# Two token blocks taken through half the hidden features each in turn, with the first layer's weights converted in pairs

## The chip, the cores and the metric

The kernel runs on one core of a Trainium2 chip. The metric is device time in microseconds (us), the median of repeated runs; smaller is better. Engines are called as in the profile: PE (matrix products) with PEld (its weight loads), DVE (vector), ACT (scalar, activations), POOL (GpSimd) and SP (here only a queue that starts DMA transfers). PSUM holds the results of PE, SBUF everything else.

## The reference, cut to what matters

```python
# q, k, v: (8, 8, 576, 64) float32; weights arrive as 64-bit floats
scores = q_c @ k_c.T / 8           # in chunks of 64 tokens
attn = softmax(scores)
x = (attn @ v_c)                   # -> (4608, 512)
h = x @ w_in                       # (512, 2048)
g = maximum(h, 0) + alpha * minimum(h, 0)
x = g @ w_out                      # (2048, 512)
h = x @ w_in2
g = h - tanh(h)
out = g @ w_out2                   # (4608, 512) float32
```

## The kernel before, in words

4608 tokens are cut into 9 blocks of 512 (`NB`), the 2048 hidden features into 16 groups of 128 (`KF`), f = 0 to 15. A **step** is one f of one block. The program runs the 9 blocks through layer 1, then the 9 blocks through layer 2: 288 steps.

Each step has two halves on PE, 12 matmuls of 128x512 each. `up` (L417) multiplies the block's input by the group's slice of w_in into one PSUM bank (`hps`). `down` (L476) multiplies the activated group by its slice of w_out and adds into four PSUM banks (`y`), which collect all 16 groups. `down` of f stands two steps after `up` of f (`LAG = 2`, a queue). For accuracy every factor is kept as a high and a low part, and a half is three products: high times high, low times high, high times low.

Between the halves stand, in layer 1: two ACT operations (`neg`, L432, and `g`, L433), a DVE operation that joins them (L434), then the split of g: the high part on ACT (`ghi`, L446), the low part on POOL or DVE (`glo`, L449).

The weights arrive as 64-bit floats, which no engine here computes with. A slice is called a piece, (f, 0) for w_in and (f, 1) for w_out, 128x512 numbers; layer 1 has 32. A piece is loaded by SP and turned into float32 by two ACT operations (`wm`, `scrh` or `scrl` at L106, `wr` at L107) and four DVE operations (L117, L121, L123, L127; together the conversion). Then it is split: high part on ACT (L152), low part on POOL (L153). All of layer 1's pieces are converted while block 0 runs, two pieces a step. Layer 2's pieces are converted during the later blocks of layer 1, written to device memory ("parked") and fetched before layer 2.

Attention works on tiles of 128 tokens, four to a block. Tiles 0 to 3 are done ahead of step 0, later tiles beside the steps: score matmuls (L284), maximum and subtraction on DVE (L313, L316), exponential on ACT (L319), sum and reciprocal on DVE (L325 to L328), the multiplication on POOL (L329), transposition and copies (L334, L343 on DVE, L344 on ACT), the product with v (L355), and the split of the result into the block's input (`xh` L397 on ACT, `xl` L401 on DVE).

The order: most of the program is written in the order in which each engine is to run it (`manual_schedule`); a table (`at`, `fire`) hangs attention, loads and conversions on step numbers. Only the steps of block 0 (`step_first`) are ordered by the framework's scheduler; `step_one` serves the other blocks of layer 1, `step_two` layer 2. An engine takes its instructions strictly in its order and waits where one isn't ready.

At a block's end `finish` copies the four banks by ACT into tiles `yst` of the pool `stage` (7 buffers of 128x512, shared with many other tiles) and SP writes them to device memory; layer 2 reads them back as `yraw`.

Of the kernel before, what the change touches and what calls it, by code (L numbers as in the profile page):

```python
# [11 lines left out]
I32 = mybir.dt.int32  # L12
# [15 lines left out]
def kernel(  # L28
# [32 lines left out]
    stage = ctx.enter_context(tc.tile_pool(name="stage", bufs=7))  # L61
# [18 lines left out]

    wsplit = {}

    def slot(f, which, shape, dtype):
        return wpool.tile(shape, dtype, tag=f"w{which}_{f}", name=f"w{which}_{f}")

    def load_raw(raw, layer, f, which, h=0):
        src = ((w_in1, w_out1), (w_in2, w_out2))[layer][which]
        n = raw.shape[1]
        if which == 0:
            nc.sync.dma_start(  # L90
                out=raw.rearrange("p (kk m) -> p kk m", m=P),
                in_=src[h * n:(h + 1) * n, f * P:(f + 1) * P].rearrange(
                    "(kk p) m -> p kk m", p=P),
            )
        else:
            nc.sync.dma_start(out=raw, in_=src[f * P:(f + 1) * P, h * n:(h + 1) * n])

    def to_f32_a(raw, m):
# [6 lines left out]
        r = stage.tile([P, 512], I32, tag="st", name="wr")[:, :raw.shape[1]]  # L105
# [23 lines left out]
    def new_w():  # L129
        return stage.tile([P, 512], F32, tag="st", name="wm")  # L130

    raw_w, w32 = {}, {}

    def load_w(f, which):
        raw_w[f, which] = slot(f, which, [P, 512], I64)
        load_raw(raw_w[f, which], 0, f, which)

    scratch, w_parts = [], {}

    def convert_a(*pieces):  # L140
# [6 lines left out]
    def convert_b(*pieces, ops=(0, 1, 2, 3)):
        to_f32_b([w_parts[piece] for piece in pieces], ops)

    def split_w(f, which, lo_engine):  # L150
        w, w_ = w32.pop((f, which)), slot(f, which, [P, 2, 512], F32R)
        nc.scalar.activation(out=w_[:, 0], in_=w, func=AF.Copy)  # L152
        lo_engine.tensor_tensor(out=w_[:, 1], in0=w, in1=w_[:, 0].bitcast(F32), op=ALU.subtract)  # L153
        wsplit[f, which] = w_

    parked, park_raw, park_t = {}, {}, {}

    def park_load(f, which, h):
        park_raw[f, which, h] = stage.tile([P, 256], I64, tag="st", name="rw")
        load_raw(park_raw[f, which, h], 1, f, which, h)  # L160

    def park_convert(f, which, h):
        if h == 0:
            park_t[f, which] = new_w()
        to_f32_b([to_f32_a(park_raw.pop((f, which, h)), park_t[f, which][:, h * 256:(h + 1) * 256])])

    def park_store(f, which):
        parked[f, which] = dram.tile([P, 512], F32, name=f"w2_{which}_{f}")
        nc.sync.dma_start(out=parked[f, which], in_=park_t.pop((f, which)))

    def fetch_w(f, which):
        w32[f, which] = new_w()
        nc.sync.dma_start(out=w32[f, which], in_=parked[f, which])
# [12 lines left out]
    def load_v(t, f=None):  # L186
        vt = slot(f[0], f[1], [P, H, D], F32) if f else vpool.tile([P, H, D], F32, tag="v", name="v")
# [66 lines left out]
    def att_a_early(t, i):  # L254
        tr = ps_y.tile([P, HP, P], F32, tag=f"y{i}", name="tr")
# [53 lines left out]
    def att_e(t, early=False):  # L309
# [4 lines left out]
        pool, tag = (stage, "st") if early else (att, "p")  # L314
        p = pool.tile([P, H, D], F32, tag=tag, name="p")
# [48 lines left out]
    def att_t_early(t):  # L364
# [5 lines left out]
        pts[t] = stage.tile([P, HP, P], F32, tag="st", name="pte")  # L370
        return nc.scalar.activation(out=pts[t], in_=tr, func=AF.Copy)
# [97 lines left out]
    def down(layer, f, g, acc, cuts=((0, 4),)):  # L469
        w = wsplit[f, 1]  # L470
        for c0, c1 in cuts:
            for i, (u, x) in enumerate(((0, 0), (1, 0), (0, 1))):
                for t in range(c0, c1):
# [3 lines left out]
                        out=acc[t], lhsT=lhsT, rhs=rhs, start=(f == 0 and i == 0), stop=(f == KF - 1 and i == 2)  # L477
# [7 lines left out]
    ysc = {}  # L485

    def finish(layer, j, t0, acc, ends=False):
        if layer == 0:
            ysc[j] = dram.tile([KD, P, NB], F32, name=f"ysc{j}")
        for i, a in enumerate(acc):  # L490
            st = stage.tile([P, 512], F32, tag="st", name="yst")
            if i % 2 == 0 or not ends:
# [324 lines left out]
```

## Time and profile before

| | us |
|---|---|
| median of 3 runs (lowest to highest) | 1712.93 (1711.82 to 1713.32) |
| the profiled execution's own time | 1713.04 |
| its span, first to last instruction | 1711.3 |
| PE busy | 1660.6 (97%) |
| DVE busy | 1300.3 (76%) |
| ACT busy | 837.4 (49%) |
| POOL busy | 354.2 (21%) |

The busy share is a mean over stages. The span in 40 slices of 43 us shows PE at nine tenths or more nearly everywhere but in the first four slices, where DVE is at nine tenths and the granted TensorE clock dips. So the views by stretch, by wait and in order of time are read for the first 185 us apart from the rest.

### The profile page before, as it was taken

The numbers are of one execution on the slowest core, as the hardware profiler recorded it, in microseconds if no ns is written. First come the engines' busy times: TensorE is split into PE (matmuls) and PEld (weight loads), VectorE is DVE, ScalarE is ACT, GpSimd is POOL, SyncE is SP. The second block draws the span as 40 slices with busy tenths as digits, with TensorE's granted clock in tenths as the row PEclk, the third lists the DMA queues.
The fourth block names the chain that finished last, engine by engine and source line by source line (L and its number), as shares of the span: only waits on it lengthen the run. The fifth ranks groups of instructions, "written<-read, shape, count | busy, mean of one in ns | idle before, by whom it ended". The sixth has DMA issues, their size and how long they took to land.

```text
span 1711.3 us, 25017 instructions
## 1 busy us (share of the span) xinstructions
PE 1660.6 (97%) x9389; PEld 1365.2 (80%) x9389; DVE 1300.3 (76%) x2000; ACT 837.4 (49%) x1593; POOL 354.2 (21%) x265
## 2 busy tenths in 40 slices
PE   7876899999999999999999999999999999999998
PEld 6664787888888888888888888888888888888887
DVE  7998465766576765664245999999999999999987
ACT  6575444555555545454355444444444444444443
POOL 2654100000000000000054322222222222222221
PEclk9897899999999999999999999999999999999999
DMA  9821323343253333430233010101010100000000
GB/s 247 255 59 28 72 69 87 93 106 87 58 121 75 102 85 93 99 88 18 94 89 108 1 50 1 50 1 50 1 50 1 41 10 27 23 19 32 6 20 25
DMA packets 215593, 108.60 MB, mean 63 GB/s; under 512 B 170912, under 2 KB 187312, under 8 KB 215472
## 3 DMA queue, kind: packets, MB, share of 16 engines
q1 hardware_dynamic: 215472, 107.01, 23.4%
q8 instruction: 73, 1.20, 0.3%
q14 instruction: 48, 0.39, 0.1%
HBM read 79.70 MB, written 27.26 MB: 63 GB/s over the span
## 4 chain that ended last, share of the span: by engine, by line
PE 83%; DVE 7%; issue 5%; POOL 2%; ACT 1%; SPq 1%; DMA 1%; POOLq 0%; DVEq 0%; ACTq 0%
PE y L476 40%; PE hps L417 40%; POOL w L153 2%; PE sc L284 1%; SPq L231 1%; PE sc L355 1%; DVE g L434 1%; DVE wm L123 1%; DVE wm L117 1%; DVE scrh L117 1%; DVE wm L127 0%; DVE scrh L123 0%; DMA wm<-w 0%; DVE wm L121 0%; DVE scrl L123 0%
## 5 line engine op out<-in xcount | busy, mean ns | idle before, releaser
L417 PE MATMUL hps<-xh,w 128*128 128x512 f32 (+1 forms) x2312 | 578.6, 392 | 11.5 <-ACT xh L397 9.2
L417 PEld LDWEIGHTS hps<-xh,w 128*128 128x128 f32 x2312 | 436.1, 189 | 103.6 <-ACT xh L397 9.5
L449 POOL TENSOR_TENSOR glo<-g,ghi 128x512 fp32r<-128x512 f32 x160 | 214.1, 1338 | 604.1 <-ACT ghi L446 560.5
L476 PE MATMUL y<-ghi,w 128*128 128x512 f32 x1152 | 304.8, 400 | 8.7 <-ACT ghi L446 5.1
L417 PE MATMUL hps<-xl,w 128*128 128x512 f32 (+1 forms) x1156 | 309.0, 389 | 0.0
L476 PE MATMUL y<-w,ghi 128*128 128x512 f32 x1152 | 293.7, 389 | 1.4 <-ACT ghi L446 1.3
L458 ACT ACTIVATE sq<-hps 128x512 f32<-128x512 f32 x144 | 86.2, 598 | 417.0 <-PE hps L417 416.1
L434 DVE SCALAR_TENSOR_TENSOR g<-neg,nalpha_sb,g 128x512 f32<-128x512 f32 x144 | 115.5, 802 | 206.9 <-ACT g L433 206.9
L476 PEld LDWEIGHTS y<-ghi,w 128*128 128x128 f32 x1152 | 216.7, 191 | 57.4 <-ACT ghi L446 6.1
L476 PEld LDWEIGHTS y<-w,ghi 128*128 128x128 f32 x1152 | 216.0, 188 | 47.4 <-ACT ghi L446 2.7
L417 PEld LDWEIGHTS hps<-xl,w 128*128 128x128 f32 x1156 | 217.3, 188 | 45.2
L465 DVE SCALAR_TENSOR_TENSOR g<-w,g 128x512 f32<-128x512 f32 x144 | 242.3, 1682 | 0.0
L446 ACT ACTIVATE ghi<-g 128x512 fp32r<-128x512 f32 x288 | 181.8, 631 | 85.1 <-DVE g L434 72.6
L432 ACT ACTIVATE neg<-hps 128x512 f32<-128x512 f32 x144 | 85.9, 597 | 213.3 <-PE hps L417 203.5
L329 POOL TENSOR_TENSOR p<-p,rd 128x512 f32<-128x512 f32 x35 | 44.6, 1274 | 604.8 <-DVE rd L328 602.4
L476 PE MATMUL y<-glo,w 128*128 128x512 f32 x576 | 163.9, 392 | 0.0
L476 PE MATMUL y<-w,glo 128*128 128x512 f32 x576 | 162.8, 389 | 0.0
L476 PEld LDWEIGHTS y<-glo,w 128*128 128x128 f32 x576 | 109.4, 190 | 23.2
L476 PEld LDWEIGHTS y<-w,glo 128*128 128x128 f32 x576 | 108.1, 188 | 22.8 <-DVE glo L449 0.4
L466 DVE SCALAR_TENSOR_TENSOR g<-sq,g 128x512 f32<-128x512 f32 x144 | 111.3, 773 | 5.0
L467 DVE COPY_PREDICATED g<-ktc,th 128x512 f32<-128x512 uint32 x144 | 109.7, 762 | 4.9
L449 DVE TENSOR_TENSOR glo<-g,ghi 128x512 fp32r<-128x512 f32 x128 | 91.9, 718 | 23.5 <-ACT ghi L446 22.6
(98 smaller groups left out, 1517.8 us busy)
## 6 DMA issues: line engine op xcount, KB each, us to landing
ysc<-yst SPq DMA_DIRECT2D x36, 256.0 KB, 2.3
yraw<-ysc SPq DMA_DIRECT2D x9, 1024.0 KB, 5.9
out_dram<-yst SPq DMA_DIRECT2D x36, 256.0 KB, 2.2
w<-in_moe_w_in_dram SPq DMA_DIRECT2D x16, 512.0 KB, 6.2
w<-in_moe_w_out_dram SPq DMA_DIRECT2D x16, 512.0 KB, 6.2
rw<-in_moe_w_in_dram SPq DMA_DIRECT2D x32, 256.0 KB, 3.0
rw<-in_moe_w_out_dram SPq DMA_DIRECT2D x32, 256.0 KB, 3.1
w<-wm SPq DMA_DIRECT2D x32, 256.0 KB, 2.1
```

Of the source, the lines that this page charges most:

```text
L117: nc.vector.tensor_scalar(out=m, in0=m, scalar1=as_float(0x4FEFFFFF), scalar2=as_float(0x40000000), op0=ALU.min, op1=ALU.max)
L329: engine.tensor_tensor(out=p, in0=p, in1=rd.to_broadcast([P, H, D]), op=ALU.mult)
L417: nc.tensor.matmul(out=hp[:, cols], lhsT=w[:, a, m], rhs=x[b][:, kk, cols], start=(kk == 0 and i == 0), stop=(kk == KD - 1 and i == 2),)
L432: nc.scalar.activation(out=neg, in_=hp, func=AF.Relu, scale=-1.0)
L434: nc.vector.scalar_tensor_tensor(out=g, in0=neg, scalar=nalpha_sb[:, f:f + 1], in1=g, op0=ALU.mult, op1=ALU.add)
L446: nc.scalar.activation(out=hi, in_=g, func=AF.Copy)
L449: lo_engine.tensor_tensor(out=lo, in0=g, in1=hi.bitcast(F32), op=ALU.subtract)
L458: nc.scalar.activation(out=sq, in_=hp, func=AF.Square)
L465: nc.vector.scalar_tensor_tensor(out=g, in0=w, scalar=ce, in1=g, op0=ALU.add, op1=ALU.mult)
L466: nc.vector.scalar_tensor_tensor(out=g, in0=sq, scalar=ca, in1=g, op0=ALU.add, op1=ALU.mult)
L467: nc.vector.copy_predicated(g, mask, th)
L476: nc.tensor.matmul(out=acc[t], lhsT=lhsT, rhs=rhs, start=(f == 0 and i == 0), stop=(f == KF - 1 and i == 2))
```

## The change

The first two blocks are taken in four parts: block 0 with f 0 to 7, block 1 with f 0 to 7, block 0 with f 8 to 15, block 1 with f 8 to 15. Between its parts a block's four `y` banks are written to device memory (`finish_half`), read back (`load_half`) and added by DVE to the sums of the second part (`finish_sum`). The parts are numbered as steps 0 to 31; the steps from 32 on are as before.

The layer-1 pieces form 15 pairs (two, (0,0) and (1,0), stay single): pair d holds (d, 1) and (d+2, 0), and each operation of its conversion and split takes 1024 columns. Pair d is converted in step d for d = 0 to 7 (`step_first`, now for 8 steps), pairs 8 to 14 in steps 9, 11, ... 21 and split one step later. A pair has one place in SBUF (`home`), which in the beginning also holds data of attention. Tiles 4 to 7 are now loaded and transposed early like tiles 0 to 3 (`att_a_second`); their attention runs in steps 1 to 7. The whole program is in written order. `stage` has 3 buffers instead of 7, a pool `wide` takes tiles of 1024, `g` has two buffers of its own. Layer 2's pieces are converted whole instead of in halves, and fetched in pairs.

```diff
-    stage = ctx.enter_context(tc.tile_pool(name="stage", bufs=7))
+    stage = ctx.enter_context(tc.tile_pool(name="stage", bufs=3))
+    wide = ctx.enter_context(tc.tile_pool(name="wide", bufs=2))
...
+    PAIRS = {"s0": [(0, 0)], "s1": [(1, 0)]}
+    PAIRS.update({d: [(d, 1), (d + 2, 0)] for d in range(KF - 2)})
+    PAIRS[KF - 2] = [(KF - 2, 1), (KF - 1, 1)]
...
+    def convert_a(d):
+        raw, m = raw_w.pop(d), new_w(d).rearrange("p a n -> p (a n)")
+        r = wide.tile([P, 1024], I32, tag="r", name="wr", bufs=1)[:, :m.shape[1]]
+        w_parts[d] = to_f32_a(raw.rearrange("p a n -> p (a n)"), m, r)
...
+    def split_w(d, lo_engine):
+        w = w32.pop(d)
+        w_ = home(d, [P, len(PAIRS[d]), 2, 512], F32R, "w")
+        nc.scalar.activation(out=w_[:, :, 0], in_=w, func=AF.Copy)
+        lo_engine.tensor_tensor(out=w_[:, :, 1], in0=w, in1=w_[:, :, 0].bitcast(F32), op=ALU.subtract)
...
-                        out=acc[t], lhsT=lhsT, rhs=rhs, start=(f == 0 and i == 0), stop=(f == KF - 1 and i == 2)
+                        out=acc[t], lhsT=lhsT, rhs=rhs, start=(f == ends[0] and i == 0), stop=(f == ends[1] and i == 2)
...
+    def finish_half(j, acc):
+        spill[j] = dram.tile([KD, P, NB], F32, name=f"half{j}")
+        put_away(acc, spill[j])
...
+    def finish_sum(j, acc):
+        ysc[j] = dram.tile([KD, P, NB], F32, name=f"ysc{j}")
+        for i, (a, y) in enumerate(zip(acc, half.pop(j))):
+            nc.vector.tensor_tensor(out=y, in0=a, in1=y, op=ALU.add)
+            nc.sync.dma_start(out=ysc[j][i], in_=y)
...
-        base[t] = (3, 5, 7, 9)[t - NPT] if t < 2 * NPT else KF * (t // NPT - 1) - 4 + 4 * (t % NPT)
+        base[t] = t - 3 if t < 2 * NPT else 2 * t + 3 if t < 3 * NPT else KF * (t // NPT - 1) - 4 + 4 * (t % NPT)
...
+    for d in range(HF, KF - 1):
+        at(2 * d - 7, convert, d)
+        at(2 * d - 6, split_w, d, nc.gpsimd)
...
+    def step_first(step, j, t0, f, ends, x, acc):
+        d, t = step, chain.get(step)
+        if late:
+            split_hi(*late[0])
+        fire(step, (1,))
+        convert_a(d)
+        if t is not None:
+            att_e(t)
+        hp = up(f, x, NB, slice(2 * P, NB), hp0) if step == 0 else up(f, x, NB)
+        fire(step, (0,))
+        if len(queue) == LAG:
+            next_down()
+        if step == 0:
+            att_a_second(5)
+        if step == 1:
+            att_a_second(6)
+            att_a_second(7)
+        convert_b(d, (0,))
+        if t is not None:
+            att_n(t)
+        if late:
+            split_lo(*late.pop(), nc.gpsimd)
+        convert_b(d, (1, 2))
+        if t is not None:
+            att_t(t)
+            att_d(t)
+        convert_b(d, (3,))
+        g = act_g(0, f, hp, NB)
+        queue.append((0, f, g, acc, j, t0, ends))
+        late.append(g)
+        split_w(d, nc.gpsimd)
+        fire(step, (2, 3, 4))
...
+    parts = [(j, a, a + HF) for a in (0, HF) for j in range(2)] + [(j, 0, KF) for j in range(2, len(plan))]
+    step = 0
+    with tc.manual_schedule():
+        for j, a, b in parts:
```

**DVE, before: around the fourth step of block 0.** `scrh`, `scrl` and `wm` are pieces in conversion, `g` the activation that PE waits for.

```order
L117 TENSOR_SCALAR scrh<-scrh 128x512
L121 TENSOR_SCALAR scrh<-scrh 128x512
L123 SCALAR_TENSOR_TENSOR scrh<-w_5_156,scrh 128x512
L127 ISA scrh<-scrh,wr 128x1024
L434 SCALAR_TENSOR_TENSOR g<-neg,nalpha_sb,g 128x512
L117 TENSOR_SCALAR scrl<-scrl 128x512
L121 TENSOR_SCALAR scrl<-scrl 128x512
L123 SCALAR_TENSOR_TENSOR scrl<-w_3_161,scrl 128x512
```

**DVE, in the change: step 2, the first with a tile's attention (tile 4), between the `g` of steps 1 and 2.**

```order
L320 TENSOR_REDUCE mx<-sc 128x8
L322 TENSOR_TENSOR p<-sc,mx 128x512
L120 TENSOR_SCALAR wm<-wm 128x1024
L331 TENSOR_REDUCE sm<-p 128x8
L333 TENSOR_SCALAR sm<-sm 128x8
L334 RECIPROCAL rd<-sm 128x8
L124 TENSOR_SCALAR wm<-wm 128x1024
L126 SCALAR_TENSOR_TENSOR wm<-raww,wm 128x1024
L340 STREAM_TRANSPOSE pt<-p 128x512
L349 COPY ptb<-pt 32x8x32 x4
L130 ISA wm<-wm,wr 128x2048
L437 SCALAR_TENSOR_TENSOR g<-neg,nalpha_sb,g 128x512
```

A step's four conversion operations now stand once, at 1024 columns, with the tile's attention dealt out between them.

**POOL, in the change: the last operations before step 1 and those of steps 1 to 3** (before, every `w` row was 128x512, and there were about two for each `glo`).

```order
L159 TENSOR_TENSOR w<-wm,w 128x2x512
L452 TENSOR_TENSOR glo<-g,ghi 128x512
L159 TENSOR_TENSOR w<-wm,w 128x2x512
L335 TENSOR_TENSOR p<-p,rd 128x512
L452 TENSOR_TENSOR glo<-g,ghi 128x512
L159 TENSOR_TENSOR w<-wm,w 128x2x512
```

A step has one split of 1024 columns, one `glo`, and the tile's multiplication ahead of `glo`.

**PE, in the change: the `up` halves of steps 7, 8 and 9 and the `down` rows that follow two of them, for the bank y0** (numbers kept: xh_166 is block 0's input, xh_832 block 1's; w_351 and w_471 hold f 0 and 1).

```order
L423 MATMUL hps_1096<-xh_166,w_1016 128x512 x8
...
L479 MATMUL y0_679<-ghi_1014,w_1016 128x512
...
L423 MATMUL hps_1144<-xh_832,w_351 128x512 x8
...
L479 MATMUL y0_679<-ghi_1081,w_1083 128x512
...
L423 MATMUL hps_1181<-xh_832,w_471 128x512 x8
```

After f = 7 of block 0 PE goes on with f = 0 of block 1, whose weights have been there since the beginning; before, the `up` of f = 8 of block 0 stood there.

## Rows read from the trace of the kernel before

**Rows 1.** Cores: span of the core and mean granted TensorE clock.

```profile
core 0: 1711.3 us, clock 0.987
```

**Rows 2.** Windows: length, busy (count) of PE, PEld, DVE, ACT, POOL; clock, DMA share, GB/s.

```profile
31.00:181.00 150.00, 112.58 (x700) 87.86 (x700) 135.99 (x193) 89.59 (x169) 76.49 (x51) 0.85 0.45 122
181.00:1711.00 1530.00, 1523.53 (x8326) 1255.61 (x8324) 1142.65 (x1759) 730.47 (x1393) 272.06 (x204) 1.00 0.20 54
```

**Rows 3.** PE's own waits, 181 to 1711 us: total, times, longest us.

```profile
PE y L476 <- ACT yst L493: 1.5, 1, 1.5
```

**Rows 4.** Chain that ended last, 176 to 188 us: start, us, what.

```profile
176.26 5.13 PE hps L417 x12
181.39 0.62 PE sc L284 x32
...
182.48 2.96 PE y L476 x12
185.44 2.72 PE hps L417 x12
```

**Rows 5.** Windows of L417 alone, then L476 alone: PE, PEld, clock, DMA, GB/s.

```profile
27.15:181.39 154.24, 57.88 (x216) 42.78 (x216) 0.86 0.47 126
27.15:181.39 154.24, 50.39 (x168) 35.73 (x168) 0.86 0.47 126
```

**Rows 6.** Timeline of DVE with POOL idle: start, us of one.

```profile
41.13 0.43 DVE L121 TENSOR_SCALAR scrl<-scrl 128x512 int32<-128x512 int32 x1
42.14 0.69 DVE L123 SCALAR_TENSOR_TENSOR scrl<-w,scrl 128x512 int32<-128x512 int32 x1
42.74 0.69 DVE L127 CUSTOM_DVE_ANT_0 scrh<-scrh,wr 128x1024 uint16<-128x1024 uint16 x1
```

**Rows 7.** Timeline of POOL, then of DVE, about 46 us.

```profile
46.24 1.46 POOL L153 TENSOR_TENSOR w<-scrh,w 128x512 fp32r<-128x512 f32 x1
46.59 1.39 DVE L121 TENSOR_SCALAR scrh<-scrh 128x512 int32<-128x512 int32 x1
```

**Rows 8.** Groups of DVE by form, 182 to 480 us: busy, mean ns | idle before.

```profile
L123 DVE SCALAR_TENSOR_TENSOR wm<-rw,wm 128x256 int32<-128x256 int32 x30 | 12.8, 425 | 1.0
L121 DVE TENSOR_SCALAR wm<-wm 128x256 int32<-128x256 int32 x30 | 8.8, 295 | 1.0
L343 DVE COPY ptb<-pt 32x256 f32<-32x256 f32 x48 | 13.7, 285 | 1.1
L313 DVE TENSOR_REDUCE mx<-sc 128x8 f32<-128x512 f32 x13 | 8.9, 684 | 0.0
L328 DVE RECIPROCAL rd<-sm 128x8 f32<-128x8 f32 x13 | 2.6, 204 | 0.4
```

**Rows 9.** Groups of ACT by form, first 182 us, the last row 182 to 480.

```profile
L106 ACT ACTIVATE wm<-w 128x512 f32<-128x512 f32 x14 | 9.3, 668 | 2.3 <-DMA w<-in_moe_w_in_dram 2.3
L152 ACT ACTIVATE w<-wm 128x512 fp32r<-128x512 f32 x13 | 8.2, 629 | 11.1 <-DVE wm L127 11.0
L106 ACT ACTIVATE wm<-rw 128x256 f32<-128x256 f32 x30 | 13.0, 434 | 0.7 <-DMA ysc<-yst 0.5
```

**Rows 10.** Timeline of POOL, 19 to 25 us: nothing beside it.

```profile
19.75 1.04 POOL L329 TENSOR_TENSOR p<-p,rd 128x512 f32<-128x512 f32 x1 [2.47 <-DMA w<-in_v_dram]
20.81 1.28 POOL L153 TENSOR_TENSOR w<-scrh,w 128x512 fp32r<-128x512 f32 x1
```

**Rows 11.** Timeline, 33 to 42 us: the end of step 0's `up`.

```profile
33.82 1.04 PE L250 MATMUL tr<-ident,w 128*128 128x128 f32 x8
35.37 0.60 ACT L432 ACTIVATE neg<-hps 128x512 f32<-128x512 f32 x1 [1.45 <-PE hps L417]
```

**Rows 12.** Timeline at a block's end in layer 2; then tile yst's landings.

```profile
1101.45 2.06 ACT L493 ACTIVATE yst<-y 128x512 f32<-128x512 f32 x4
...
1106.62 0.62 PE L476 MATMUL y<-w,ghi 128*128 128x512 f32 x2
DMA to landing us min/median/max: 2.0/2.2/4.4
```

More of the change, by code (lines that the diff above doesn't have):

```diff
@@ L147, in convert_b @@
[L147 to L160, printed above, removed]
@@ new lines, in load_w, with new_w @@
+    def load_w(d):
+        raw_w[d] = home(d, [P, len(PAIRS[d]), 512], I64, "raww")
+        for i, (f, which) in enumerate(PAIRS[d]):
+            load_raw(raw_w[d][:, i], 0, f, which)
+    def new_w(d):
+        w32[d] = wide.tile([P, 2, 512], F32, tag="w", name="wm")[:, :len(PAIRS[d])]
+        return w32[d]
+    def convert_a(d):
+        raw, m = raw_w.pop(d), new_w(d).rearrange("p a n -> p (a n)")
+        r = wide.tile([P, 1024], I32, tag="r", name="wr", bufs=1)[:, :m.shape[1]]
+        w_parts[d] = to_f32_a(raw.rearrange("p a n -> p (a n)"), m, r)
@@ L369, in att_t_early @@
             nc.tensor.transpose(tr[:, hp, :], p[:, hp * P:(hp + 1) * P], ident)
-        pts[t] = stage.tile([P, HP, P], F32, tag="st", name="pte")
-        return nc.scalar.activation(out=pts[t], in_=tr, func=AF.Copy)
+        pts[t] = first_pt[:, t]
+        nc.scalar.activation(out=pts[t], in_=tr, func=AF.Copy)
     def att_v_early(t):
@@ L467, in tanhshrink, with down @@
         nc.vector.copy_predicated(g, mask, th)
-    def down(layer, f, g, acc, cuts=((0, 4),)):
+    def down(layer, f, g, acc, ends, cuts=((0, 4),)):
         w = wsplit[f, 1]
@@ L483, in new_acc, with finish, put_away @@
         return [ps_y.tile([P, DM], F32, tag=f"y{i}", name=f"y{i}") for i in range(n // P)]
-    ysc = {}
-    def finish(layer, j, t0, acc, ends=False):
+    ysc, spill, half = {}, {}, {}
+    def finish(layer, j, t0, acc, last=False):
         if layer == 0:
             ysc[j] = dram.tile([KD, P, NB], F32, name=f"ysc{j}")
+        put_away(acc, ysc[j] if layer == 0 else [out[t0 + i * P:t0 + (i + 1) * P, :] for i in range(KD)], last)
+    def put_away(acc, to, last=False):
         for i, a in enumerate(acc):
             st = stage.tile([P, 512], F32, tag="st", name="yst")
-            if i % 2 == 0 or not ends:
+            if i % 2 == 0 or not last:
                 nc.scalar.activation(out=st, in_=a, func=AF.Copy)
@@ L495, in finish, with load_half @@
                 nc.vector.tensor_copy(st, a)
-            nc.sync.dma_start(out=ysc[j][i] if layer == 0 else out[t0 + i * P:t0 + (i + 1) * P, :], in_=st)
+            nc.sync.dma_start(out=to[i], in_=st)
+    def finish_half(j, acc):
+        spill[j] = dram.tile([KD, P, NB], F32, name=f"half{j}")
+        put_away(acc, spill[j])
+    def load_half(j):
+        half[j] = []
+        for i in range(0, KD, 2):
+            two = wide.tile([P, 2, 512], F32, tag="w", name="yhalf")
+            nc.sync.dma_start(out=two, in_=spill[j][i:i + 2].rearrange("kk p t -> p kk t"))
+            half[j] += [two[:, 0], two[:, 1]]
+    def finish_sum(j, acc):
[3 more added lines that the diff above has]
+            nc.sync.dma_start(out=ysc[j][i], in_=y)
     yraw = {}
@@ L753, in step_one @@
             split_lo(*late.pop(), nc.vector)
+        hp = up(f, x, NB)
+        fire(step, (0,))
+        done = next_down()
         fire(step, (3,))
         g = act_g(0, f, hp, NB)
-        queue.append((0, f, g, acc, j, t0))
+        queue.append((0, f, g, acc, j, t0, ends))
         late.append(g)
-        if j == 1 and f == 0:
-            split_w(KF - 1, 1, nc.gpsimd)
         if done:
```

299 lines of the change are left out of this document (137 added, 162 removed).

## The prediction

> **What bounds the kernel now.** The first look is at the span and clock of the one core [rows 1]: 1711.3 us at 0.987, so a little of the time ran below full clock. The windows [rows 2] say where. From 31 to 181 us PE is busy 112.6 of 150 us at a clock of 0.85, and DVE is busy 136.0, over nine tenths; from 181 us on PE is busy 1523.5 of 1530 at a clock of 1.00. The reader should see two stages with different limits. In the second only work on PE counts: its waits there [rows 3] come to one notable one, of 1.5 us. In order of time [rows 4], an `up` half takes 5.13 us up to 181.4, at the end of the first stage, and two steps' halves later 2.72. So 2.72 us is the price of a half once PE is fed.
>
> How much was done by then is counted [rows 5]: 216 matmuls of `up` (24 of them half as wide, the first step's) are 17 halves, 168 of `down` are 14. These 31 halves would take 84.3 us at 2.72, and took from 27 to 181. The difference, some 70 us less the attention of that stretch, is what the change can reach for. Attention there is tiles 4 to 8: at 0.62 us [rows 4] for each of two products and 1.04 [rows 11] for the transposition, 11 us for five tiles. So some 59 us at most.
>
> What holds the first stage is seen between DVE and POOL. With POOL idle a conversion operation with one input takes 0.43 us and one with two 0.69, and the next starts 0.60 later [rows 6]. While POOL runs, the 0.43 becomes 1.39: it starts at 46.59, and ends at 47.98, 0.28 after POOL's at 47.70 [rows 7]. Such an operation and POOL's don't share time, they take turns. The Trainium skill (SBUF — State Buffer, section "Who interferes with whom") has it as a lock that whichever starts first holds for its whole instruction, and leaves reductions out of it; the trace agrees for the conversion [rows 7]. If that lock were the only limit, the sum would be 1680 us, the first rival below.
>
> **The early steps, part by part.** First the prices at 1024 columns, which the trace lacks. From 256 columns to 512, the one-input operation goes from 0.295 to 0.43 us and the two-input one from 0.425 to 0.69 [rows 6, 8]; carried on, 1024 gives 0.70 and 1.22, and less the 0.09 by which operations overlap, 0.61 and 1.13. A pair's conversion is twice each: 3.48 us, against 3.76 for two pieces (0.34 and 0.60 apiece, twice each, twice). The wide form alone thus saves 0.3 us a pair. The same step on ACT [rows 9] takes 0.434 to 0.668, so 1.1 at 1024; the high split, 0.63 at 512, I also take at 1.1. POOL's split takes 1.28 at 512 with nothing beside it [rows 10]; I take twice that, 2.56. Bounds: 1.28 more or less a fixed part that no row shows, so 2.3 to 2.9 with 0.3 either way.
>
> Now a step of the first eight, as a chain from the end of the pair's last conversion operation to the next pair's. ACT splits (1.1), POOL splits (2.56): at 3.66 DVE gets its first operation in (0.61, to 4.27). POOL's `glo` is next in turn (1.28, to 5.55), then DVE's other three (0.61, 1.13, 1.13): 8.4 us. `g`, 0.6 on DVE, lies beside ACT's 1.1 at the start.
>
> With a tile's attention (steps 2 to 5), ACT comes to the exponential at 1.1 + 0.63 + 1.1 + 1.1 + 0.63 = 4.56; then the sum (0.6, about the 0.68 of a reduction in [rows 8] less the overlap) and two tiny operations (0.2 each): 5.55 by rounding. Then DVE's second operation to 6.16, POOL's multiplication (1.04 [rows 10]) to 7.2, the third to 8.33, `glo` to 9.61 with the transposition beside it, four copies at 0.285 [rows 8] to 10.75, the last to 11.9. In steps 4 and 5 the earlier tiles' `xh` and `xl` push the exponential back by about 0.5: 12.4. Steps 6 and 7 have that too, but no exponential to wait for: 8.4.
>
> Steps 1 to 7 are 3 x 8.4 + 2 x 11.9 + 2 x 12.4 = 73.8 us. They begin with the high split of pair 0, which stands in ACT's order behind step 0's `neg` and `g`. Before, `neg` started at 35.37 [rows 11]. The change puts four copies of tiles 4 and 5 ahead of it, and `neg` takes 0.60, 0.5 with the overlap; at 0.5 for each of the six operations that is 3.0: 38.5 with rounding, give or take 2. The loads are early enough: up to pair 3 they are some 10.5 MB, fewer than before by the same step, so I cost them nothing; what hides them is the wait for the conversions before.
>
> So pair 7 is converted at 112.3 and split by POOL at 116.0. By then PE has done `up` of steps 0 to 9 and `down` of steps 0 to 6, for `up` of steps 8 and 9 takes weights that are there since the beginning: 17 halves. From there it is fed. To where the old trace stands at 182.5 it has 31 - 17 = 14 halves left, 38.1 us, and tile 8's transposition (1.04 [rows 11]) and three products (0.62 each): 2.9. That is 157.0.
>
> **What follows.** The other seven pairs (8 to 14) lie in 13 steps, 6.0 us of DVE and POOL per two steps of 10.9 us, which the halves hide. It is tight in steps 19 to 22, where tiles 8 and 9 fall in, and in 19 and 20 the DVE transpositions of tiles 9 and 10. DVE has 3.48 us for a pair, 2.4 for two `g` and two `glo`, 4.5 for a tile's attention (five operations near 0.6, two tiny ones, the copies) and 2.4 for four transpositions, 12.8, and in taking turns POOL's 2.56 and 1.04: 16.4 in two steps, against 12.1 on PE (four halves and two products). In the next two, without the transpositions, 14.0. The lag of 6.2 us is about what the queue of two steps can give; I take 1.5 us of waiting, between 0 and 6.2. Adding the halves' sums costs DVE four operations of 0.69, the writing four copies on ACT, each beside PE. PE's work after that is the same.
>
> 157.0 + 1.5 = 158.5, 24.0 before 182.5. The span becomes 1687.3. The profiled execution took 1713.0 for a span of 1711.3, and the median stands 0.1 below it, so **1689 us**.
>
> **The rivals.** *The turns alone:* if ACT's part is hidden, a step costs what DVE and POOL need in turn: 3.48 + 0.60 + 1.28 + 2.56 = 7.9, with attention 1.04 + 1.14 + 0.2 more, 10.3. Steps 1 to 7 are 65 us, and the end 1680. For it: the first stage of before, with DVE over nine tenths busy [rows 2]. Against: there the scheduler mixed two or three pieces, here the order is fixed and a single pair is in hand, so DVE has nothing to do while ACT prepares it.
>
> *Nothing overlaps:* if besides that all the reductions, the exponential and ACT's 2.2 us a step stand in the chain, it is some 95 us, 22 more than forecast: 1711, no gain. It would take a step of 13.6 on the mean.
>
> *A slow clock:* PE has 5.4 to 6.7 us of work in an early step of 8.4 to 12.4. If the granted clock stays at the lower of its two levels (1.2 and 2.4 GHz) there, a half costs 5.13 [rows 4], a step 10.3 and its attention about 1. That lies inside steps 2 to 5, but steps 6 and 7 grow by 2.4 each, and the lead of three halves at 116 is lost, 8.2: 1702. For it: 0.85 over the first stage [rows 2], with PE busier than it will be. Against: in steps 6 and 7, the shortest, PE is busy two thirds of the time. The Trainium skill (TensorE: Matmul & The Clock Gate, Part 1, "The HAM clock gate") has the engine fall to half rate after idling and return once it is busy; no row here shows which of the two these steps will be.
>
> *Waits at every block's end, the one that ends slower:* `yst` has 3 buffers now, so the fourth copy of a block waits until the first has landed. In layer 2 the copies start at 1101.45 and PE wants the fourth bank at about 1106.62 [rows 12]. A copy of 0.61, a landing of 2.2 and a copy more end 3.0 to 3.5 us after the start, and with the longest landing, 4.4, at 5.7, half a microsecond late. Before, the one such wait cost PE 1.5 us [rows 3]. At 1.5 us at each of 17 ends it is 25.5: 1714.5, and above 1.6 the change is slower by more than 0.2%. Against it: the median landing leaves 1.7 us to spare, and the activations `g` no longer take buffers of `stage`.
>
> **How the numbers follow.** The forecast, 1677 to 1700 by the 2 us of the start, the price of POOL's split (0.3 x 7) and the 0 to 6.2 of the tight steps, with the turns alone at its lower part: 0.66. The slow clock 0.12. Nothing overlaps 0.09. The block's ends 0.07. Below 1677, by a start or a mixture that I price too high: 0.06. The range that holds it 8 times in 10 goes from 1677 to 1703 and takes in the slow clock. A measurement tells 0.2%, 3.4 us, from no change: faster are the first two, the last and part of the third, 0.88; within 0.2%, 0.05; slower, 0.07.
>
> **What would show it.** Right: DVE's wide operations near 0.7 and 1.2 us where POOL is idle; POOL's wide split near 2.6; the first `up` of block 1 before 116 us, and PE nearly without a gap from then on at full clock; steps of 8 to 9 us without attention and 12 to 13 with it. Wrong: `up` of block 1 later than 125 us, the lower clock beyond 116, PE waiting for `yst` at most block ends, or waiting in steps 19 to 27 by more than 6 us.

## The result, and the profile after

The change takes 1695.32 us in the median (1693.4 to 1697.62, 4 runs) against 1712.66 before (1711.82 to 1713.32, 4 runs): a ratio of 0.990, with a 95% interval of 0.9882 to 0.9917. That is 17.3 us less. The profiled execution is the longest of the four, 1697.62 us, with a span of 1695.8; against the old span it is 15.5 us shorter. The sums below go by the profiled execution, so 2.3 us of what they miss is only its distance to the median.

The cores view of after, which answers to [rows 1]:

```profile
core 0: 1695.8 us, clock 0.991
```

The windows of after, which answer to [rows 2] in finer steps (length, then busy time and count of PE, PEld, DVE, ACT and POOL; clock, DMA share, GB/s):

```profile
60.00:80.00 20.00, 12.98 (x156) 10.77 (x157) 17.10 (x26) 12.14 (x18) 10.16 (x6) 0.70 0.31 110
80.00:100.00 20.00, 14.35 (x109) 11.27 (x107) 16.03 (x26) 13.96 (x23) 10.19 (x6) 0.84 0.73 256
100.00:120.00 20.00, 20.00 (x95) 16.41 (x88) 15.82 (x15) 11.14 (x19) 7.99 (x4) 0.94 0.00 1
120.00:180.00 60.00, 60.00 (x299) 49.54 (x298) 44.09 (x47) 38.33 (x57) 12.00 (x5) 1.00 0.35 93
180.00:240.00 60.00, 54.98 (x473) 44.21 (x472) 49.33 (x81) 30.64 (x57) 10.10 (x6) 1.00 0.38 97
```

The first stage still is DVE's: 17.10 of 20 us in the first row, with PE at 12.98 and the clock at 0.70. But it is over at 100 us; from there to 180 PE has no gap. Before, PE was busy 112.6 of the 150 us from 31 to 181. A new soft place lies between 180 and 240 us, where PE lacks 5.0 us. PE's waits from 95 to 300 us, one line each (start, length, what; in brackets the idle time before it and what ended it):

```profile
99.16 1.13 PE L361 MATMUL xp<-ptb,v 64*64 64x64 f32 x32 [2.73 <-issue]
198.17 0.69 PE L291 MATMUL sc<-ktc,qt 64*64 64x64 f32 x32 [1.61 <-DVE p L322]
212.65 0.69 PE L291 MATMUL sc<-ktc,qt 64*64 64x64 f32 x32 [2.18 <-DVE ktc L276]
232.46 0.69 PE L291 MATMUL sc<-ktc,qt 64*64 64x64 f32 x32 [1.23 <-DVE xl L407]
```

The last early wait ends at 99.16, before tile 7's product with v. The other three, 5.0 us together, are score products in steps 23, 25 and 28, of tiles 10, 11 and 12.

Where the gain stands along the program can be read from SP's first copy at a block's end, which marks the same point of the work in both kernels. First two such rows of the old kernel (blocks 2 and 8, the blocks counted from 0), then the same two of the new one:

```profile
377.20 2.06 SPq L496 DMA_DIRECT2D ysc<-yst  x4
927.64 3.72 SPq L496 DMA_DIRECT2D ysc<-yst  x4
```

```profile
357.60 3.10 SPq L502 DMA_DIRECT2D ysc<-yst  x4
910.06 3.04 SPq L502 DMA_DIRECT2D ysc<-yst  x4
```

The gain is 19.6 us at block 2's end, 17.6 at block 8's and 15.5 at the last instruction (1711.3 less 1695.8). So 4.1 us are given back in a stretch whose work was to be the same: 2.0 from block 2's end to block 8's, 2.1 after that.

The early steps, marked by ACT's high split of each pair's 1024 columns, pairs 0 to 7 (the timeline of ACT in after; pairs 2 to 4, at 60.52, 72.00 and 84.13, are left out):

```profile
38.41 1.08 ACT L158 ACTIVATE w<-wm 128x1024 fp32r<-128x1024 f32 x1
49.12 1.07 ACT L158 ACTIVATE w<-wm 128x1024 fp32r<-128x1024 f32 x1
...
96.27 1.06 ACT L158 ACTIVATE w<-wm 128x1024 fp32r<-128x1024 f32 x1
104.67 1.06 ACT L158 ACTIVATE w<-wm 128x1024 fp32r<-128x1024 f32 x1 [3.28 <-DVE wm L130]
113.13 1.06 ACT L158 ACTIVATE w<-wm 128x1024 fp32r<-128x1024 f32 x1 [3.34 <-DVE wm L130]
```

The distances are 10.7, 11.4, 11.5, 12.1, 12.1, 8.4 and 8.5 us, 74.7 in all. One step without attention, from the timeline of after, DVE and POOL between two of these splits (`g` ahead of them is left out):

```profile
97.40 2.37 POOL L159 TENSOR_TENSOR w<-wm,w 128x1024 fp32r<-128x1024 f32 x1 [3.58 <-ACT w L158]
98.36 0.69 DVE L407 TENSOR_TENSOR xl<-xp,xh 128x512 fp32r<-128x512 f32 x1 [1.33 <-ACT xh L403]
99.39 0.93 DVE L120 TENSOR_SCALAR wm<-wm 128x1024 f32<-128x1024 f32 x1 [0.34 <-ACT wm L109]
99.72 1.74 POOL L452 TENSOR_TENSOR glo<-g,ghi 128x512 fp32r<-128x512 f32 x1
100.36 1.65 DVE L124 TENSOR_SCALAR wm<-wm 128x1024 int32<-128x1024 int32 x1
102.05 1.22 DVE L126 SCALAR_TENSOR_TENSOR wm<-raww,wm 128x1024 int32<-128x1024 int32 x1
103.41 1.23 DVE L130 CUSTOM_DVE_ANT_0 wm<-wm,wr 128x2048 uint16<-128x2048 uint16 x1
```

The chain of the forecast is there in its order: ACT's split, POOL's split to 99.77, DVE's first operation stretched to 0.93 until POOL lets go, POOL's `glo` behind it, the second operation stretched to 1.65, and the last two at their own length.

### The profile page after: what moved, and what is told of

It reads as the page before. It is cut to its first block, busy times and chain, and to the rows that moved or that the text cites. A ratio compares the mean times of both kernels' runs of the same rounds, so it can differ in the third digit from the quotient of the medians.

```text
span 1695.8 us, 24503 instructions
## 1 busy us (share of the span) xinstructions
PE 1655.5 (98%) x9389; PEld 1364.4 (80%) x9389; DVE 1280.6 (76%) x1825; ACT 820.5 (48%) x1473; POOL 324.2 (19%) x226
## 4 chain that ended last, share of the span: by engine, by line
PE 87%; DVE 5%; SPq 2%; ACT 2%; DMA 2%; issue 1%; DVEq 0%; ACTq 0%
PE y L479 43%; PE hps L423 42%; PE sc L291 1%; DVE g L469 1%; SPq L200 1%; PE sc L361 1%; SPq L195 1%; DMA raww<-in_moe_w_out_dram 0%; DVE g L468 0%; DMA ysc<-yst 0%; DVE wm L126 0%; DMA first<-in_k_dram 0%; DVE g L437 0%; SPq L95 0%; DMA v<-in_v_dram 0%
## 5 line engine op out<-in xcount | busy, mean ns | idle before, releaser
L423 PE MATMUL hps<-xh,w 128*128 128x512 f32 (+1 forms) x2312 | 570.7, 389 | 0.0
L452 POOL TENSOR_TENSOR glo<-g,ghi 128x512 fp32r<-128x512 f32 x151 | 200.0, 1324 | 579.9 <-ACT ghi L449 579.9
L437 DVE SCALAR_TENSOR_TENSOR g<-neg,nalpha_sb,g 128x512 f32<-128x512 f32 x144 | 110.4, 767 | 193.8 <-ACT g L436 193.6
L452 DVE TENSOR_TENSOR glo<-g,ghi 128x512 fp32r<-128x512 f32 x137 | 112.5, 821 | 39.4 <-ACT ghi L449 38.6
L159 POOL TENSOR_TENSOR w<-wm,w 128x1024 fp32r<-128x1024 f32 (+1 forms) x34 | 79.4, 2335 | 213.1 <-ACT w L158 201.5
```

The costliest lines, as they stand in the source:

```text
L159: lo_engine.tensor_tensor(out=w_[:, :, 1], in0=w, in1=w_[:, :, 0].bitcast(F32), op=ALU.subtract)
L423: nc.tensor.matmul(out=hp[:, cols], lhsT=w[:, a, m], rhs=x[b][:, kk, cols], start=(kk == 0 and i == 0), stop=(kk == KD - 1 and i == 2),)
L437: nc.vector.scalar_tensor_tensor(out=g, in0=neg, scalar=nalpha_sb[:, f:f + 1], in1=g, op0=ALU.mult, op1=ALU.add)
L452: lo_engine.tensor_tensor(out=lo, in0=g, in1=hi.bitcast(F32), op=ALU.subtract)
```

## The experiments

Each was timed beside the kernel before on the same chip (median 1713.87 us for the first four kernels, 1712.84 for the next four, 1712.28 for the last two), so the ratios are what compares. No kernel with more buffers for `yst` was run, so what the `yst` waits would cost with more or fewer of them stays open.

**Experiment 1: the change without its halves.** Wide pairs, written order and early tiles stay; block 0 takes all 16 features at once.

```diff
-    parts = [(j, a, a + HF) for a in (0, HF) for j in range(2)] + [(j, 0, KF) for j in range(2, len(plan))]
+    parts = [(j, 0, KF) for j in range(len(plan))]
...
-                fn = step_two if layer else step_one if step >= HF else step_first
+                fn = step_two if layer else step_one if step >= KF - 1 else step_first
```

> The change without its halves: block 0 takes features 0 to 15 in steps 0 to 14 with one pair a step, in the same fixed order, then block 1; no partial sums through device memory. Theory (the halves are what feeds PE early): steps 8 to 14 stay 8.4 us long, as steps 6 and 7 of the change are in its trace, so PE loses about 3 us in each of seven steps that the halves give it back; PE is fed from about 175 us and the time is 1706 to 1712 us, most of the gain lost. Rival (pairs and the fixed order carry the gain, the halves only move work): no more than 4 us behind the change, 1693 to 1699.

Measured: 1711.92 us (1709.47 to 1713.4, 11 runs), ratio 0.999 (0.9981 to 0.9999). POOL's splits of this kernel (two of nine in a row at the same distance), and PE's waits from 100 to 200 us:

```profile
104.86 2.41 POOL L159 TENSOR_TENSOR w<-wm,w 128x1024 fp32r<-128x1024 f32 x1 [4.34 <-ACT w L158]
113.31 2.40 POOL L159 TENSOR_TENSOR w<-wm,w 128x1024 fp32r<-128x1024 f32 x1 [4.34 <-ACT w L158]
```

```profile
PE hps L423 <- POOL w L159: 8.1, 7, 1.3
PE hps L423 <- ACT w L158: 4.7, 5, 1.1
```

A pair comes every 8.4 us to the end of the conversions at 175, while a step of PE's work takes 5.4, so PE waits for weights, 12.8 us in twelve waits. Nearly all of the gain is the halves: they don't make the conversion faster, they give PE sixteen steps from the first eight pairs. That is shown on top of the pairs and the written order; no run has the halves without them.

**Experiment 2: the pairs' operations at 512 columns again.** Everything else of the change stays.

```diff
-        w_parts[d] = to_f32_a(raw.rearrange("p a n -> p (a n)"), m, r)
+        n = len(PAIRS[d])
+        w_parts[d] = [to_f32_a(raw[:, i], m[:, i * 512:(i + 1) * 512], r[:, i * 512:(i + 1) * 512]) for i in range(n)]
```

and `split_w` likewise, piece by piece.

> The change with every conversion and split operation of a layer-1 pair, and the splits of the fetched layer-2 pairs, issued as two of 512 columns one after the other; order and halves stay. Theory (a chain of turns between DVE and POOL, priced by columns): a pair costs 0.28 us more on DVE, about 0.2 more on POOL (2.37 measured against twice 1.28) and some 0.3 more on ACT, so a step of the first seven is 0.5 to 0.8 us longer and the time is 1698 to 1702. Rival 1 (a short POOL operation lets DVE in sooner, so narrow is as good or better): 1690 to 1696. Rival 2 (the width carries the gain): above 1704.

Measured: 1699.67 us (1699.5 to 1701.27, 5 runs), ratio 0.9922 (0.9909 to 0.9934). POOL's splits, two of the eight, each now two operations:

```profile
73.74 2.50 POOL L162 TENSOR_TENSOR w<-wm,w 128x512 fp32r<-128x512 f32 x2 [5.46 <-ACT w L160]
87.19 2.50 POOL L162 TENSOR_TENSOR w<-wm,w 128x512 fp32r<-128x512 f32 x2 [5.46 <-ACT w L160]
```

By POOL's starts a step with attention takes 12.9 to 13.5 us (11.4 to 12.1 in after), one without 7.5 to 7.9 (the last three start at 100.65, 108.13 and 116.00; 8.4 in after), since POOL can start after half of ACT's split. As expected, the wide form is worth some 4 us here: the intervals of the two ratios overlap, but in the profiled executions block 2 ends 3.4 us later (361.01 for 357.60). The expected reason did not show, since the steps are not all 0.5 to 0.8 us longer. Its shorter operations, 0.3 us a pair by the forecast's working, don't make that up; the rest may be how the pieces fall between POOL's and the attention's operations, which no run tests by itself.

**Experiment 3: pairs 11 to 14 converted earlier,** in steps 14, 15, 16, 17 instead of 15, 17, 19, 21, away from the tiles of steps 19 on.

```diff
-    for d in range(HF, KF - 1):
-        at(2 * d - 7, convert, d)
-        at(2 * d - 6, split_w, d, nc.gpsimd)
+    for d, step in {8: 9, 9: 11, 10: 13, 11: 14, 12: 15, 13: 16, 14: 17}.items():
+        at(step, convert, d)
+        at(step + 1, split_w, d, nc.gpsimd)
```

> The change with pairs 11 to 14 converted in steps 14, 15, 16 and 17 instead of 15, 17, 19 and 21 (each split one step later). Theory: the three waits of PE for DVE at 198, 212 and 232 us (1.6, 2.2 and 1.2 us) come from DVE's backlog, for the conversions of pairs 13 and 14 meet the attention of tiles 8 to 10 there; without them in that place the first two waits go and the time is 3 to 5 us less, 1690 to 1693. Rival (DVE's waits within a tile's attention set them, its own turn with POOL and ACT): the waits stay and the time is within 1 us of the change, 1694 to 1697.

Measured: 1695.93 us (1694.68 to 1696.48, 4 runs), ratio 0.9897 (0.9882 to 0.9912): the rival's figure, though not for its reason. The three waits at 198, 212 and 232 us are gone; in their place PE waits for `glo`, 0.89 us at 161.81 and

```profile
169.29 0.50 PE L479 MATMUL y<-glo,w 128*128 128x512 f32 x1 [1.71 <-DVE glo L452]
178.58 1.20 PE L479 MATMUL y<-glo,w 128*128 128x512 f32 x4 [1.33 <-DVE glo L452]
```

Of 5.0 us 3.9 came back. Conversions in five steps running (13 to 17) build the same lag on DVE as a conversion and a tile do.

**Experiment 4: tiles 6 and 7 loaded first.** In after, PE waits for tile 6 in step 1:

```profile
43.21 0.63 PE L260 MATMUL tr<-ident,first 128*128 128x128 f32 x4 [2.93 <-DMA first<-in_q_dram]
```

Its load is issued behind those of `v` for tiles 4 and 5, three transfers, which hold SP for 5.9 us; SP comes to tile 6 at 36.25:

```profile
29.19 5.92 SPq L195 DMA_DIRECT2D v<-in_v_dram  x3
```

```diff
         load_first(5)
+        load_first(6)
+        load_first(7)
+        load_w(2)
         load_v(4, first_v[:, 2])
         load_v(5, first_v[:, 3])
-        load_w(2)
-        load_first(6)
-        load_first(7)
         load_w(3)
```

> The change with the loads of tiles 6 and 7 moved ahead of v of tiles 4 and 5 and of pair 2. Theory: step 1 takes 10.7 us between the high splits of pairs 0 and 1 instead of 8.4, because the copies of tile 6 stand ahead of that split in ACT's order and tile 6 lands at 43.2 us; landing some 3 us earlier it takes 8.4 to 9 and the time is 1.5 to 2.5 us less, 1692.5 to 1694.5. Rival (pair 2 then lands late, or the loads are held back together): step 2 grows by as much, or tile 6 lands no earlier, 1694.5 to 1697.

Measured: 1694.51 us (1693.71 to 1696.18, 4 runs), ratio 0.9891 (0.9878 to 0.9905). The high splits of pairs 0 and 1:

```profile
37.70 1.08 ACT L158 ACTIVATE w<-wm 128x1024 fp32r<-128x1024 f32 x1
46.16 1.06 ACT L158 ACTIVATE w<-wm 128x1024 fp32r<-128x1024 f32 x1 [1.81 <-DVE wm L130]
```

Step 1 is 8.5 us instead of 10.7, like any step without attention. The 2.2 us are shown in the trace, and block 2 ends at 354.91, 2.7 earlier; of the ratios alone, 0.0009 apart with overlapping intervals, it couldn't be told. The hold is not a fixed price of the `v` loads: behind the moved loads, at 37.53, the same three transfers hold SP for 1.98 us. The next kernels all have this edit.

**Experiment 6: seven pairs in two of three steps.** (Number 5, the kernel with more buffers, was not run.)

```diff
+    for d, step in {8: 9, 9: 10, 10: 12, 11: 13, 12: 15, 13: 16, 14: 18}.items():
```

in place of the same line of experiment 3.

> The change with tiles 6 and 7 loaded first, and pairs 8 to 14 converted in steps 9, 10, 12, 13, 15, 16, 18. Theory (DVE's backlog in the steps with a pair and a tile makes the waits of 5.0 us in steps 19 to 27, and made the 3.9 us of the early conversions): DVE and POOL in turn need some 7.0 us in a step with a pair and 1.2 in one without, 15.3 in three steps, against 16.3 or more of PE; no lag builds up, PE's waits between 140 and 240 us fall under 1.5 us, and the time is 1690 to 1692 us. Rival (the waits only move again): 3 us or more of PE's waits stay between 140 and 240 us, 1693 to 1696.

Measured: 1692.23 us (1691.91 to 1692.84, 4 runs), ratio 0.9878 (0.9863 to 0.9893). PE's waits from 100 to 300 us, in one line:

```profile
PE y L479 <- DVE glo L452: 2.3, 1, 2.3
```

Between the two theories: the three waits are gone, and one of 2.3 us stands in for them, at 136, after the pair of conversions in steps 9 and 10, when PE's own lead is still small (that reason is argued, not shown).

**Experiments 7, 8 and 9: ACT's first operation a step early, alone, with experiment 6, and with the fetched pairs split on DVE.** In 7 and 8 the operation `wm` (L109) for pair d + 1 is issued in step d, ahead of `neg`; 9 adds the last line below.

```diff
         convert_b(d, (3,))
+        if d + 1 < HF:
+            convert_m(d + 1)
         g = act_g(0, f, hp, NB)
...
         at(s, fetch_w, d)
-        at(s + 2, split_w, d, nc.gpsimd)
+        at(s + 2, split_w, d, nc.vector)
```

> The change with tiles 6 and 7 loaded first, and ACT's first operation of a pair's conversion issued a step early, ahead of neg. Theory (a chain: ACT's high split, its first operation for the next pair and only then DVE set an early step): DVE's first operation runs while ACT still splits the pair before, steps without attention shrink from 8.4 to about 7.8 us and those with it from 11.5 to about 10.8, the high split of pair 7 comes some 4 us earlier, and the time is 1689.5 to 1692 us. Rival (DVE and POOL in turn set the step, whatever ACT does): steps stay at 8.4 and 11.5 us within 0.2, 1693.5 to 1696.

> All three edits: tiles 6 and 7 first, conversions in two of three steps, ACT's first operation early. If both theories hold the gains add, 1686 to 1689 us; if PE's start and the tight steps are the same slack counted twice, it is the time of the better of the two alone, 1689.5 to 1692.

> All three edits, and the low split of layer 2's fetched pairs on DVE instead of POOL. Theory (POOL's wide splits hold up DVE and so the activation in the last block of layer 1 and the first of layer 2): PE's three waits of 0.5 us for ghi after 900 us go, 1.0 to 1.5 us less than all three edits alone. Rival: the waits stay and the time is the same within 0.5 us, since ACT's extra splits make them.

Measured: 1697.75 us for 7 (1697.09 to 1698.58, 4 runs; ratio 0.991, 0.9895 to 0.9925), 1696.06 for 8 (1695.07 to 1698.22, 4 runs; 0.9901, 0.9884 to 0.9917), 1694.82 for 9 (1693.01 to 1695.58, 4 runs; 0.9891, 0.9877 to 0.9906). Experiment 7 is slower than either theory allowed, and by the traces slower than experiment 4 (block 2 ends at 358.45, for 354.91; the intervals of the ratios overlap); 8 missed both its figures with it. ACT of experiment 7 at the end of a step with attention, after DVE's last operation on the pair (the early operation is L153 there, the high split L165):

```profile
94.53 1.23 DVE L131 CUSTOM_DVE_ANT_0 wm<-wm,wr 128x2048 uint16<-128x2048 uint16 x1
94.83 1.15 ACT L153 ACTIVATE wm<-raww 128x1024 f32<-128x1024 f32 x1
...
96.83 1.07 ACT L165 ACTIVATE w<-wm 128x1024 fp32r<-128x1024 f32 x1
...
98.93 0.69 DVE L414 TENSOR_TENSOR xl<-xp,xh 128x512 fp32r<-128x512 f32 x1 [1.20 <-ACT xh L410]
99.54 1.35 DVE L121 TENSOR_SCALAR wm<-wm 128x1024 f32<-128x1024 f32 x1
```

DVE is done with the pair at 95.76, but the split waits behind the early operation and `neg` and `g` until 96.83. In experiment 4 the same two moments are 93.16 and 93.35. So at that place ACT is on the chain, and 1.1 us put there lengthens a step with attention: 13.0 us against 12.1 for the last of them. Nor did DVE begin earlier in the next step, since `g` and `xl` stand ahead of the first operation in its order, and then POOL has started. The place was wrong; whether the chain was, is experiment 11's question.

9 against 8 came out as expected in the medians, 1.2 us less, but the intervals overlap, and the trace decides. The three waits for `ghi` between 900 and 960 us, 1.5 us in after and in 8, are gone; from block 2's end to the last instruction 9 takes 1335.6 us (1692.1 less 356.51) and 8 1337.5 (1694.7 less 357.18). The reason is in this piece of after's timeline, in the first block of layer 2:

```profile
930.17 2.85 POOL L159 TENSOR_TENSOR w<-wm,w 128x1024 fp32r<-128x1024 f32 x1
930.80 2.78 DVE L469 SCALAR_TENSOR_TENSOR g<-sq,g 128x512 f32<-128x512 f32 x1
...
934.45 0.63 ACT L449 ACTIVATE ghi<-g 128x512 fp32r<-128x512 f32 x1 [3.08 <-DVE g L470]
935.13 2.11 PE L479 MATMUL y<-w,ghi 128*128 128x512 f32 x8 [0.49 <-ACT ghi L449]
```

POOL's wide split holds an operation of the activation for 2.78 us, which takes 0.69 where POOL is idle (the same line of experiment 10):

```profile
923.48 0.69 DVE L469 SCALAR_TENSOR_TENSOR g<-sq,g 128x512 f32<-128x512 f32 x1
```

**Experiment 10: another order of the seven pairs, and the fetched pairs on DVE.** Experiment 4's loads, and

```diff
+    for d, step in {8: 9, 9: 11, 10: 12, 11: 14, 12: 15, 13: 17, 14: 18}.items():
...
+        at(s + 2, split_w, d, nc.vector)
```

> The change with tiles 6 and 7 loaded first, pairs 8 to 14 converted in steps 9, 11, 12, 14, 15, 17, 18 (no two in a row before step 11), and layer 2's fetched pairs split on DVE. Theory (DVE's backlog after two conversions in a row is what left PE 2.3 us of waiting for glo at 136 us): that wait goes, PE waits 1 us or less between 110 and 300 us, and the ghi waits after 900 us fall to 1.0: 1689 to 1691.5 us. Rival (each schedule of these seven pairs leaves PE 2 us or more somewhere): 1692 or more.

Measured: 1689.48 us (1688.34 to 1690.78, 4 runs), ratio 0.9864 (0.9849 to 0.9879). The waits from 100 to 300 us:

```profile
PE sc L291 <- DVE p L322: 1.0, 1, 1.0
PE y L479 <- DVE glo L452: 0.9, 1, 0.9
```

1.9 us together, over the 1 us expected and just under the rival's 2; the wait at 136 is gone, and of the `ghi` waits after 900 us one of 1.0 is left, as expected. In time it is where the theory had it, with an interval below that of the change (0.9882 to 0.9917). The span is 8.5 us shorter than after's (the medians 5.8). By the block ends of the profiled executions 2.7 of that is the loads (block 2 ends at 354.91 in experiment 4, for 357.60), 3.3 the order of the pairs (351.65), and the other 2.5 lies after block 2, where the split on DVE is.

**Experiment 11: the first operation early on both engines, in the right places.** Experiment 10, and

```diff
         if t is not None:
             att_e(t)
+        if d + 1 < HF:
+            convert_m(d + 1)
...
         convert_b(d, (3,))
+        if d + 1 < HF:
+            m = w32[d + 1].rearrange("p a n -> p (a n)")
+            to_f32_b([(m, m.bitcast(I32), None, None)], (0,))
         g = act_g(0, f, hp, NB)
```

> The kernel with tiles first, conversions at 9, 11, 12, 14, 15, 17, 18 and the fetched splits on DVE, and besides that ACT's first operation for the next pair right behind the exponential, with DVE's first operation of that pair right behind the last one of the pair before, ahead of g. Theory (in steps without attention the order split on ACT, split on POOL, first operation on DVE is the chain, and the early operation was only misplaced in the run before): the first operation lies beside ACT's split, steps without attention are 7.7 to 7.9 us instead of 8.4, those with attention stay within 0.3 us, and the time is 1.5 to 2 us under the kernel without it. Rival (POOL and DVE make the step in turns whatever the order): 8.4 us a step and the same time within 0.5 us.

Measured: 1688.58 us (1686.28 to 1689.37, 4 runs), ratio 0.9857 (0.984 to 0.9873). The high splits of pairs 6 and 7 (pair 5's is at 90.99), and DVE's first operation beside the former:

```profile
98.54 0.69 DVE L121 TENSOR_SCALAR wm<-wm 128x1024 f32<-128x1024 f32 x1
98.66 1.06 ACT L165 ACTIVATE w<-wm 128x1024 fp32r<-128x1024 f32 x1 [2.00 <-DVE wm L131]
...
106.37 1.06 ACT L165 ACTIVATE w<-wm 128x1024 fp32r<-128x1024 f32 x1 [1.95 <-DVE wm L131]
```

Steps without attention are 7.7 us, as the chain said, and the rival (8.4 whatever the order) is out. Those with attention were to stay within 0.3 us: two are about 1 us shorter than in experiment 10 (10.4 and 10.6 for 11.4 and 11.5), two 0.2 longer (12.3). Yet pair 7's split comes 3.45 us earlier than in experiment 10 (109.82 there), and the median falls by 0.9 only, not the 1.5 to 2 expected and less than the runs can tell. PE's last early wait ends 1.7 us earlier (94.13 for 95.85), and block 2 0.9 earlier (350.72 for 351.65): from the last tile's product on PE has weights enough, and the last two conversions don't set its pace any more. The lower clock takes a part back: the eight `down` matmuls behind that wait, from 95.19, and the four after them take 3.78 and 1.79 us, in experiment 10, from 96.80, 3.32 and 1.07. This is the fastest kernel of the study; that it is faster than the change is shown, that it is faster than experiment 10 is not.

## Why the prediction was right, and where its sum was off

The sign, the mechanism and the range held. The forecast was a gain of 24.0 us, the profiled execution shows 15.5 and the median 17.3.

**What held.** The prices at 1024 columns: 0.69 and 1.22 us on DVE with POOL idle (0.70 and 1.22 foretold), 1.06 to 1.17 on ACT (1.1), 2.37 to 2.41 on POOL in the first 200 us (2.56 taken, 2.3 the lower bound). The start: the high split of pair 0 at 38.41 (38.5). The chain: 8.4 us without attention (8.4), 11.4 to 12.1 with it (11.9 and 12.4); steps 1 to 7 take 74.7 us (73.8). That their sum comes so near is in part luck: step 1 is 2.3 us longer than foretold, and the four steps with attention are 1.4 shorter together. The first `up` of block 1 starts at 109.47 (before 116). The halves as the source of the gain: experiment 1 loses nearly all of it. The "turns alone" rival (7.9 and 10.3 us a step) fell with the same rows, and experiment 11 shows where the difference lay, in an operation that a fixed order left behind POOL's split.

**The slow clock** came as far as 0.70 from 60 to 80 us and 0.84 to 100, with PE busy 65% and 72% of the time; there it lay inside the steps of DVE. Behind the last early wait it cost something. From 99.16 on PE has no gap, so each of its delays lasts; the granted clock was 0.61 from 99.10 to 103.10 and 1.00 from there to 116. The first eight `down` matmuls of the one stretch and of the other:

```profile
100.22 3.05 PE L479 MATMUL y<-ghi,w 128*128 128x512 f32 x8
106.75 1.98 PE L479 MATMUL y<-ghi,w 128*128 128x512 f32 x8
```

With tile 7's product (1.13 us, where one at full clock, at 224.87, takes 0.69) that is 1.5 us, not the 8.2 of the rival: the lead of three halves was shortened, not lost. The trace agrees with what the prediction named from the Trainium skill (TensorE: Matmul & The Clock Gate, Part 1, "The HAM clock gate"): the clock is low behind PE's waits and full once PE is busy without a gap.

**The loads, costed at nothing.** "What hides them is the wait for the conversions before" failed for tile 6: SP reached its load at 36.25, PE had it at 43.21, and step 1 was 10.7 us instead of 8.4. Experiment 4 takes that 2.2 back. The megabytes had been counted, not the time for which SP was held by the `v` loads ahead. In the trace of after 16.4 halves were done at 116 us (101 of `up`'s 128x512 matmuls and one half at half width, 84 of `down`'s), not 17, 1.6 us of PE's work. No single term made that: the slow step 1 (2.3 us) and the lower clock (1.5) stand against the shorter steps with attention (1.4).

**The tight steps,** taken at 1.5 us of 0 to 6.2: measured 5.0, and in steps 23, 25 and 28, behind steps 19 to 22 that the sum held for tight. "The lag of 6.2 us is about what the queue of two steps can give" was too kind, for the score products stand in PE's order ahead of any queue: they wait for `p` and `ktc` on DVE directly. Experiments 3, 6 and 10 show that the lag is real work of DVE and POOL that wants room. Conversions in five steps running gave 3.9 us of waiting back, in two of three steps 2.3, in the order of experiment 10 1.9.

**"PE's work after that is the same"** was the term that was left out: 4.1 us are given back after block 2. About 2 of it goes when the fetched pairs are split on DVE instead of POOL, as experiments 9 and 10 show: from block 2's end to the last instruction the three kernels with that split on DVE take 1335.3 to 1335.7 us, those with the wide split on POOL 1337.3 to 1338.4, and before it was 1334.1 (1711.3 less 377.20). POOL's split holds an operation of the activation; the prediction had used this lock for the first eight steps and not for the second place where the pairs are split. That the change doubled the operation's width is only a part of it. Experiment 2, which splits the fetched pairs on POOL in two operations of 512 columns, still has 1.0 us of the 1.5 us of `ghi` waits between 900 and 960 us; the old kernel, with narrow splits on POOL in the same stretch, had 0.3. What makes up that difference isn't shown. PE's waits in after from 300 us to the end are these:

```profile
PE y L479 <- ACT ghi L449: 2.5, 4, 1.0
PE y L479 <- ACT yst L499: 1.7, 1, 1.7
```

Of the `ghi` waits the longest, 1.0 us, is at the program's very end, as in the kernel before (at 1704.14). The other line answers the rival that ends slower: one notable wait for `yst`, of 1.7 us, where [rows 3] has one of 1.5, not one at each of 17 ends. It lies at block 4's end, from 548.98 to 550.63, and is most of the 2.0 us lost from block 2's end to block 8's. The old one ended at 290.38, before block 2's end, and is gone.

After block 8 the `ghi` waits are most of the 2.1 us (1.5 for 0.3 before). Another 0.7 is the rival's own mechanism at the last block's end: in the chain that ended last, the fourth `yst` copy, at 1692.09, waits for the first to land, and from the start of PE's last matmul to the last instruction it is 4.95 us; before, that copy follows PE's last product at once (1707.49), and it is 4.24. The rest, half a microsecond or so, I haven't settled.

So of the 8.5 us that the profiled gain lacks, 3.5 are the tight steps, 1.6 the start and 4.1 the later blocks. The old kernel's `yst` wait, which is gone, gave 1.5 back; 0.8 is then left that I didn't trace.

## What to carry to other kernels

When a conversion holds up the main engine, look for an order in which it can do twice the work with what is converted: that gave some 15 us here, the wider instructions some 4. A lag that an engine builds up can move with another order instead of going away; count its work over windows of two or three steps, with all that it must wait for, before moving anything. When an instruction is made wider, follow it to every place where it runs, and see there which engine it holds up; here, of 1.5 us of waits, moving it to another engine took away all and narrow operations on the same engine 0.5.

## What the runs showed of the hardware

Which DVE operations POOL holds up depends on the operation and its inputs. Beside a split of POOL from 97.40 to 99.77 us, `xl`, which has one input in PSUM, took its 0.69 us (98.36, in the first section). The activation's last-but-one operation, with two inputs in SBUF, took 2.78. The Trainium skill (SBUF — State Buffer, "Who interferes with whom") says that an operation with two SBUF inputs contends and one with at most one does not, outside a mode in which `tensor_scalar` takes both ports; the rows agree with both halves. Not expected was how small an operation can be and still be held for the whole of POOL's instruction: the `tensor_scalar` of 8 columns (DVE, then POOL, timelines of after), 0.17 us by itself (at 89.71):

```profile
186.52 2.01 DVE L333 TENSOR_SCALAR sm<-sm 128x8 f32<-128x8 f32 x1
```

```profile
186.10 2.40 POOL L159 TENSOR_TENSOR w<-wm,w 128x1024 fp32r<-128x1024 f32 x1 [10.34 <-ACT w L158]
```

It ends at 188.53, POOL's at 188.50, and a tile's softmax waits for it.
